# A ring with a copied head, and a maximum that is written back in place

## The chip, the cores and the metric

The kernel runs on one core of one Trainium2 chip. The metric is the device time of one execution in microseconds, lower is better. The core has five engines with a queue each: TensorE for matrix products (PE, with its weight loads shown apart as PEld), VectorE (DVE), ScalarE (ACT), GpSimd (POOL) and SyncE (SP). In this kernel SP does no arithmetic: its queue issues every DMA, one after the other, in the order of the program, and an issue that has to wait holds up all issues behind it.

## The reference

Two branches read the same input `x` (2048 tokens, 512 features, 32-bit floats) and a sigmoid gate per token mixes them.

```python
# attention branch, H = 32 heads of 16, window W = 256
q, k, v = split(x @ wqkv)
scores = q @ k.T * 16 ** -0.5
mask = (i - j >= 0) & (i - j < 256)
o = softmax(where(mask, scores, -1e9)) @ v
a = o @ wo
# gated branch, F = 1376
b = (sigmoid(x @ w_gate) * (x @ w_up)) @ w_down
g = sigmoid((x * gate_w).sum(-1))
out = g * a + (1 - g) * b
```

## The kernel before

**Precision.** Each 32-bit operand is split into a high and a low part, and a product is made of three matrix products, high by high, high by low and low by high. For the projections they are three passes. For the scores they are folded into one pass: the 64 rows of one head in a stack hold 16 rows for each of four terms. Row group 0 of a query block carries minus the row maximum and of a key block the constant one; groups 1 to 3 hold high and low parts of queries and keys (three pairings).

**The ring.** `ring_t` (lines 95 and 96) holds three stacks (`RING = 3`) of 8 blocks of 128 tokens each, 24 blocks. A free index of four says which of queries (0, 1) and keys (2, 3) and which pair of heads; the two heads of a pair lie in rows 0 to 63 and 64 to 127. Stacks are numbered t = 0 to 15. There are eight groups of four heads with 16 blocks each, so a group has two stacks, and stack t lies in third t % 3 of the ring. `stack_build` (line 287) lists 13 DMAs for a stack: one that zeroes the rows of the maximum, and 12 that copy high and low parts from two staging tiles, 32 rows each, first the eight of the high parts and then the four of the low parts.

**Units.** The loop of line 657 runs over units u = 0 to 139. Up to u = 127, unit u is block u % 16 of group u // 16. For each of four heads hh, `s_part` (line 317) multiplies the query block with the key blocks u-2 to u into PSUM, and one DVE instruction adds the mask and takes the maximum per row (line 332); its elementwise result goes to the tile `junk`, which nobody reads, and the maximum to `mx`. The PSUM tile has the tag `s`, of which there are two. `st_part` (line 366) does the same with keys and queries swapped, nine units later (`LAG`), with the maximum in row group 0, and ACT takes the exponential. `pv_burst` makes the product with `v` every four units. Between the heads, `run_slots` puts in the matrix products of the gated branch and of later projections (lines 563 to 576), so that PE has something to do at every point. All engines but POOL run in the order of the program text.

**The cut.** Because the ring has 24 blocks, a run of three blocks can cross its end. `pieces` (line 306) cuts it there, and `s_part` and `st_part` then make two matmuls with the same weights. That is the case at u = 24 and 25, 72 and 73, 120 and 121 for the scores, and nine units after the two blocks before each of these crossings for the transposed ones (block 22 comes up in `st_part` at u = 31, block 23 at u = 32).

**The order of the DMAs.** At u = 10 and then at every u with u % 8 == 1 from 17 on, the variable `sdma` is set to the list of stack u // 8 + 1 (line 673). In each unit the program emits, in this order: the reload of `v` or of projection weights, the load of maxima (`max_load`, where u % 4 == 1), the stores that the unit before left in `later`, then up to three (`SD = 3`) DMAs of `sdma` (lines 674 to 682), and then the heads. In units with u % 4 == 0 the four stores of the maxima (`max_store`, line 717) come after the third head; they wait for a transpose on DVE, and the `max_load` of the next unit waits for these stores to land, since it reads them back from memory.

**After the attention.** The softmax sums are stored, read back into the tile `sm` (line 623, two buffers), inverted on DVE and stored again as `rec_scratch`, once per quarter of the tokens. The loads of the quarters are emitted at u = 127, 131, 135 and 139. The last loads of the sums, of the gate row (line 745) and of the hidden blocks (`h_load`, line 600) stand in one row on the SP queue, and the final stage, lines 788 to 830, begins with the hidden blocks.

Of the kernel before, what the change touches and what calls it, by code (L numbers as in the profile page):

```python
# [7 lines left out]
F32 = mybir.dt.float32  # L8
F32R = mybir.dt.float32r
# [5 lines left out]
P = 128  # L15
# [25 lines left out]
NEG = -1.0e30  # L41

RING = 3
CH2 = 2 * CH
LAG = 9
PVLAG = LAG + 2
SD = 3
QB = 32
# [10 lines left out]
def gated_mix_kernel(  # L59
# [11 lines left out]
    nc = tc.nc  # L71
    ctx.enter_context(tc.manual_schedule(engines={E.PE, E.Activation, E.SP, E.DVE}))

    mm = nc.tensor.matmul
# [15 lines left out]
    max_d = nc.dram_tensor("max_scratch", (NG * NC, HG, 2, 4, P), F32, kind="Internal").ap()  # L90
    fill_d = nc.dram_tensor("fill_scratch", (2, CH2), F32, kind="Internal").ap()

    cpool = ctx.enter_context(tc.tile_pool(name="cpool", bufs=1))
    ps = ctx.enter_context(tc.tile_pool(name="ps", bufs=1, space=PSUM))
    ring_t = cpool.tile([P, 4, RING * CH2], F32R, name="ring")
    ring = [ring_t[:, :, r * CH2:(r + 1) * CH2] for r in range(RING)]
    gsum = cpool.tile([P, NB], F32, name="gsum")
    gs = cpool.tile([P, NB], F32, name="gs")
# [3 lines left out]
    def ring_f(f):  # L102
        t = ring[(NP - 3 + f // 4) % RING]
        return t[:, f % 4, 0:D], t[:, f % 4, D:]
# [24 lines left out]
    with ExitStack() as actx:  # L129
        apool = actx.enter_context(tc.tile_pool(name="apool", bufs=1))  # L130
        xh = apool.tile([P, ND, T], F32R, name="xh")
        xl = apool.tile([P, ND, T], F32R, name="xl")
        w0 = apool.tile([P, 2, CH2], F32R, name="w0")

# [5 lines left out]
        spool = actx.enter_context(tc.tile_pool(name="spool", bufs=2))  # L140
# [35 lines left out]
        def fill_rows(r, which, v):  # L176
            dst = ring[r].bitcast(F32).rearrange("(a r) j f -> r a j f", r=32)[0, :, 2 * which:2 * which + 2]
            return dst, fill_d[v:v + 1].partition_broadcast(8).rearrange("(a j) o f -> a j (o f)", j=2)

        warm = cpool.tile([P, CH2], F32R, tag="hb", name="warm", bufs=4)  # L180
        nc.vector.memset(warm[:, 0:2 * P].bitcast(F32), 0.0)
# [19 lines left out]
        mask = apool.tile([P, 3 * P], F32, name="mask")  # L201
# [8 lines left out]
        )  # L210
        fr = cpool.tile([P, CH2], F32, tag="hb", name="fr", bufs=4)
        nc.gpsimd.memset(fr[0:33], 0.0)
        nc.gpsimd.memset(fr[32:33], 1.0)
        nc.sync.dma_start(fill_d, fr.rearrange("(a r) f -> r a f", r=32)[0, 0:2])
        for r in range(RING):
            nc.gpsimd.memset(ring[r].bitcast(F32), 0.0)
            nc.sync.dma_start(*fill_rows(r, 1, 1))

        def fill_v(b0, b1):
            nc.gpsimd.memset(Vh[:, b0:b1, :, DH:VW], 1.0)  # L220

        fill_v(0, NB // 2)

        vp = {}
# [62 lines left out]
        def stack_build(t):  # L287
            sh, sl = (v.bitcast(F32) for v in stg.pop(t))
            rt = ring[t % RING].bitcast(F32)
            st = rt.rearrange("(a r) j f -> r a j f", r=4)  # L290
            dmas = [fill_rows(t % RING, 0, 0)]
            for low in range(2):
                for j in range(4):
                    for r in range(3):
                        if low == (r == (1 if j < 2 else 2)):
                            dmas.append((st[r + 1, :, j], (sl if low else sh)[32 * j:32 * j + 32]))
            return dmas

        def run_dmas(dmas):
# [2 lines left out]

        def pos(g, b):
            return (g * NB + b) % (8 * RING)

        def pieces(g, b0, b1):
            cut = b0 + 8 * RING - pos(g, b0)
            return [(b0, b1)] if cut >= b1 else [(b0, cut), (cut, b1)]

        def blk(g, b, hh, which, n=1):  # L310
            base = 64 * (hh % 2)
            o = pos(g, b) * P
            return ring_t[base:base + 64, which * 2 + hh // 2, o:o + n * P]
# [3 lines left out]
        def s_part(u, hh):  # L317
            g, i = divmod(u, NB)
            s = g * NC + i // 4
            if i % 4 == 0 and hh == 0:  # L320
                mxs[s] = spool.tile([P, HG, 4], F32, tag="mx", name=f"mx{s}")
            k0 = max(0, i - 2)
            pt = ps.tile([P, 3 * P], F32, tag="s", name=f"s{u}_{hh}", bufs=2)
            lhsT = blk(g, i, hh, 0)
            for k, e in pieces(g, k0, i + 1):
                mm(  # L326
                    pt[:, (k - k0) * P:(e - k0) * P], lhsT, blk(g, k, hh, 1, e - k),
                    start=k == k0, stop=e == i + 1, skip_group_check=True,
                )
            n = (i + 1 - k0) * P  # L330
            junk = spool.tile([P, 3 * P], F32, tag="junk", name=f"junk{u}_{hh}", bufs=2)
            nc.vector.tensor_tensor_reduce(  # L332
                junk[:, 0:n], pt[:, 0:n], mask[:, 3 * P - n:], scale=1.0, scalar=NEG,
                op0=ALU.add, op1=ALU.max, accum_out=mxs[s][:, hh, i % 4:i % 4 + 1],
            )

# [20 lines left out]
        def max_load(s):  # L357
            st = ring[s // 2 % RING].bitcast(F32).rearrange("(a r) j f -> r a j f", r=QB)
            o = s % 2 * CH
            nc.sync.dma_start(  # L360
                st[0, :, 0:2, o:o + CH], max_d[s].rearrange("(p s) l b t -> (s l) p (b t)", p=2),
            )

        pts = {}

        def st_part(u, hh):
            g, j = divmod(u, NB)
            if u not in pts:
                o = PSLOT[u] * PW
                pts[u] = region[:, o:o + PW].rearrange("p (h q) -> p h q", h=HG)  # L370
            tag, bufs = ("s", 2) if u + LAG >= NU else ("st", 3)
            pt = ps.tile([P, 3 * P], F32, tag=tag, name=f"st{u}_{hh}", bufs=bufs)
            lhsT = blk(g, j, hh, 1)
            last = min(NB, j + 3)
            for q, e in pieces(g, j, last):
                mm(  # L376
                    pt[:, (q - j) * P:(e - j) * P], lhsT, blk(g, q, hh, 0, e - q),
                    start=q == j, stop=e == last, skip_group_check=True,
                )
            n = (last - j) * P  # L380
            nc.scalar.activation(pts[u][:, hh, 0:n], pt[:, 0:n], AF.Exp, scale=SCALE)  # L381

        def mask_p(u):
# [87 lines left out]
        proj(0)  # L471
        proj(1)
        run_dmas(stack_build(0))
        split_x(2)
        split_wqk(1, raw_q)
        v_block(4)
        split_x(3)
        fill_v(NB // 2, NB)
        v_block(5)
        proj(2)  # L480
        v_block(6)
        proj(3)
        run_dmas(stack_build(1))
        v_block(7)
        v_block(8)
# [132 lines left out]
        sm = {}  # L618

        def flat(v, c):  # L620
            return v[c].rearrange("h (q t) -> (h q) t", t=P)

        def sums_load(c):
            sm[c] = cpool.tile([P, P], F32, tag="sm", name=f"sm{c}", bufs=2)
            nc.sync.dma_start(sm[c], flat(sum_d, c))

        def sums_invert(c):
# [23 lines left out]
        while w < NU:  # L651
            n = BURST if w + 8 < NU else 2
# [4 lines left out]
        for u in range(N):  # L657
# [15 lines left out]
            if (u % 8 == 1 and u > 16 or u == LAG + 1) and u // 8 + 1 < NP:  # L673
                sdma = stack_build(u // 8 + 1)
            if u % 16 == 8 and u // 16 + 2 < NG:
                raw_q = load_wqk(u // 16 + 2)
            if u % 4 == 1 and 1 < u <= NU + 1:
                max_load(u // 4 - 1)
# [17 lines left out]
            for hh in range(HG):  # L696
                if hh == 0 and u % 2 == 0:
                    if u in bursts:
                        pv_burst(*bursts[u])
                if hh == 0:  # L700
                    head = min(2, bursts.get(u, (0, 0))[1] // 2)
                    run_slots(head)
                if u < NU:
                    s_part(u, hh)
                if 0 <= u - LAG < NU:
                    st_part(u - LAG, hh ^ 1 if u < NU else hh)
                if u < LAG:
                    flush(behind)
                    run_slots(GAP)
                    flush(acts)  # L710
                    flush(behind)
                else:
                    if behind:
                        behind.pop(0)()
                    if acts:
                        acts.pop(0)()
                if hh == 2 and u % 4 == 0 and 0 < u <= NU:
                    max_store(u // 4 - 1)
                if u >= LAG:
                    run_slots((GAP if u >= NU else GAPS[u % 4][hh] if u > LAG + 2 else GAP * (u % 2 == 0 or hh < HG - 1)) - (hh < head))  # L720
# [10 lines left out]
            if SUMS <= u and (u - SUMS) % 4 == 0:  # L731
                sums_load((u - SUMS) // 4)
# [55 lines left out]
        for n, (c, f) in enumerate(steps):  # L788
# [31 lines left out]
            for t in range(4):  # L820
                b = 4 * c + t
# [61 lines left out]
```

## Time and profile before

| | |
|---|---|
| time, median of 3 runs | 728.19 us (727.78 to 728.48) |
| time of the profiled execution | 728.12 us |
| its span, first to last instruction | 726.4 us |
| PE busy | 720.6 us, 99% |
| PEld busy | 594.1 us, 82% |
| DVE busy | 461.2 us, 63% |
| ACT busy | 438.0 us, 60% |
| POOL busy | 166.9 us, 23% |
| mean granted TensorE clock | 0.999 |
| DMA packets | 88,656 on SP's queue, 111.39 MB |

The span leaves out 1.7 us of the profiled execution's own time, before the first and after the last instruction. PE runs two matmuls at once, each on half of the rows, and their records overlap, so the busy time says that there is nearly always a matmul under way and not that each one runs as fast as it can. How long a piece of work takes on PE is therefore read from the distance between starts.

### The profile page before, as it was taken

The numbers are of one execution on the slowest core, as the hardware profiler recorded it, in microseconds if no ns is written. First come the engines' busy times: TensorE is split into PE (matmuls) and PEld (weight loads), VectorE is DVE, ScalarE is ACT, GpSimd is POOL, SyncE is SP. The second block draws the span as 40 slices with busy tenths as digits, with TensorE's granted clock in tenths as the row PEclk, the third lists the DMA queues.
The fourth block names the chain that finished last, engine by engine and source line by source line (L and its number), as shares of the span: only waits on it lengthen the run. The fifth ranks groups of instructions, "written<-read, shape, count | busy, mean of one in ns | idle before, by whom it ended". The sixth has DMA issues, their size and how long they took to land.

```text
span 726.4 us, 20432 instructions
## 1 busy us (share of the span) xinstructions
PE 720.6 (99%) x7775; PEld 594.1 (82%) x7775; DVE 461.2 (63%) x1426; ACT 438.0 (60%) x899; POOL 166.9 (23%) x256
## 2 busy tenths in 40 slices
PE   9999999999999999999999999999999999999997
PEld 7888788888888878878888788888886788888886
DVE  4447867757776676766776677666415868557471
ACT  6412876667677677667667677666767545435241
POOL 7000433332233233232323323323330000000000
PEclk9999999999999999999999999999999999999999
DMA  9382564445455355345545435644464959366441
GB/s 319 97 267 85 144 167 136 137 133 139 125 151 136 109 148 156 120 122 154 137 129 135 134 100 151 187 134 151 151 187 144 272 188 276 126 227 190 150 138 58
DMA packets 88753, 112.68 MB, mean 155 GB/s; under 512 B 36050, under 2 KB 45778, under 8 KB 88656
## 3 DMA queue, kind: packets, MB, share of 16 engines
q1 hardware_dynamic: 88656, 111.39, 52.2%
q8 instruction: 61, 1.00, 0.6%
q14 instruction: 36, 0.29, 0.1%
HBM read 49.72 MB, written 36.45 MB: 119 GB/s over the span
## 4 chain that ended last, share of the span: by engine, by line
PE 96%; DMA 1%; DVE 1%; SPq 0%; issue 0%; ACT 0%; DVEq 0%; ACTq 0%
PE gu L259 38%; PE pj L259 10%; PE pvs L430 8%; PE st L376 6%; PE s L326 6%; PE pd L83 5%; PE pd L81 5%; PE pd L82 5%; PE vps L241 3%; PE pa L81 2%; PE pa L83 2%; PE pa L82 2%; PE pvst L430 2%; PE vps L82 1%; PE vps L83 1%; PE vps L81 1%
## 5 line engine op out<-in xcount | busy, mean ns | idle before, releaser
L332 DVE CUSTOM_DVE_ANT_0 junk<-s,mask 128x384 f32<-128x384 f32 (+2 forms) x512 | 267.5, 530 | 148.3 <-PE st L376 91.6
L259 PE MATMUL gu<-xh,w 64*128 64x512 f32 (+2 forms) x1392 | 357.7, 395 | 0.0
L381 ACT ACTIVATE region<-st 128x384 f32<-128x384 f32 (+2 forms) x512 | 242.4, 476 | 92.1 <-PE st L376 42.1
L259 PE MATMUL gu<-xl,w 64*128 64x512 f32 (+2 forms) x696 | 247.1, 393 | 0.0
L259 PEld LDWEIGHTS gu<-xh,w 64*128 64x128 f32 (+2 forms) x1392 | 203.1, 183 | 22.4 <-issue 6.9
L386 POOL TENSOR_SCALAR_AFFINE_SELECT region<-region 128x512 f32<-128x512 f32 x128 | 85.5, 668 | 369.9 <-ACT region L381 283.9
L376 PE MATMUL st<-ring 64*128 64x384 f32 (+2 forms) x536 | 167.6, 320 | 0.0
L326 PE MATMUL s<-ring 64*128 64x384 f32 (+2 forms) x536 | 167.1, 321 | 0.5 <-DVE mx L332 0.5
L259 PEld LDWEIGHTS gu<-xl,w 64*128 64x128 f32 (+2 forms) x696 | 123.2, 183 | 6.3 <-issue 0.6
L326 PEld LDWEIGHTS s<-ring 64*128 64x128 f32 x536 | 98.4, 184 | 22.0 <-DVE mx L332 12.8
L376 PEld LDWEIGHTS st<-ring 64*128 64x128 f32 x536 | 98.3, 184 | 7.1 <-ACT region L381 0.2
L259 PE MATMUL pj<-xl,wqh 64*128 64x512 f32 (+1 forms) x240 | 95.2, 402 | 0.0
L259 PE MATMUL pj<-xh,wqh 64*128 64x512 f32 (+1 forms) x240 | 93.3, 394 | 0.0
L259 PE MATMUL pj<-xh,wql 64*128 64x512 f32 (+1 forms) x240 | 75.0, 392 | 0.0
L430 PE MATMUL pvs<-region,vg 64*32 64x320 f32 (+4 forms) x1440 | 73.4, 345 | 0.0
L391 POOL TENSOR_SCALAR_AFFINE_SELECT region<-region 128x512 f32<-128x512 f32 x112 | 71.9, 642 | 0.0
L430 PE MATMUL pvst<-region,vg 64*32 64x320 f32 (+4 forms) x1440 | 71.7, 340 | 0.0
L83 PE MATMUL pd<-ring,hb 128*128 128x512 f32 (+1 forms) x176 | 69.1, 392 | 0.3 <-DVE hb L78 0.3
L81 PE MATMUL pd<-ring,hb 128*128 128x512 f32 (+1 forms) x176 | 69.3, 394 | 0.0
L82 PE MATMUL pd<-ring,hb 128*128 128x512 f32 (+1 forms) x176 | 68.5, 389 | 0.0
L430 PEld LDWEIGHTS pvs<-region,vg 64*32 64x32 f32 x1440 | 45.1, 106 | 26.4 <-issue 4.0
L77 ACT CAST hb<-region 128x512 fp32r<-128x512 f32 (+1 forms) x37 | 23.0, 621 | 50.0 <-DVE region L616 41.3
(83 smaller groups left out, 1031.3 us busy)
## 6 DMA issues: line engine op xcount, KB each, us to landing
gu_scratch<-sp SPq DMA_DIRECT2D x80, 256.0 KB
region<-gu_scratch SPq DMA_DIRECT2D x68, 256.0 KB
ring<-sh SPq DMA_DIRECT2D x128, 128.0 KB
ring<-sl SPq DMA_DIRECT2D x64, 128.0 KB
guraw<-in_wgu_dram SPq DMA_DIRECT2D x20, 256.0 KB
v_scratch<-region SPq DMA_DIRECT2D x16, 272.0 KB
vg<-v_scratch SPq DMA_DIRECT2D x8, 544.0 KB
region<-in_xT_dram SPq DMA_DIRECT2D x16, 256.0 KB
```

The costliest lines, as they stand in the source:

```text
L77: nc.scalar.copy(hi, src)
L81: mm(ps, lh, rh, start=first, stop=False)
L82: mm(ps, lh, rl, start=False, stop=False)
L83: mm(ps, ll, rh, start=False, stop=last)
L259: mm(pt[0:fw], (wl if w == 2 else wh)[r, d], (xl if w == 1 else xh)[r, d, c * CH:(c + 1) * CH], start=k == 0 and half != 1, stop=k == 3 * ...
L326: mm(pt[:, (k - k0) * P:(e - k0) * P], lhsT, blk(g, k, hh, 1, e - k), start=k == k0, stop=e == i + 1, skip_group_check=True,)
L332: nc.vector.tensor_tensor_reduce(junk[:, 0:n], pt[:, 0:n], mask[:, 3 * P - n:], scale=1.0, scalar=NEG, op0=ALU.add, op1=ALU.max, accum_out ...
L376: mm(pt[:, (q - j) * P:(e - j) * P], lhsT, blk(g, q, hh, 0, e - q), start=q == j, stop=e == last, skip_group_check=True,)
L381: nc.scalar.activation(pts[u][:, hh, 0:n], pt[:, 0:n], AF.Exp, scale=SCALE)
L386: nc.gpsimd.affine_select(p[:, :, 0:P], p[:, :, 0:P], pattern=[[0, HG], [1, P]], compare_op=ALU.is_ge, fill=0.0, base=0, channel_multiplie ...
L391: nc.gpsimd.affine_select(p[:, :, 2 * P:], p[:, :, 2 * P:], pattern=[[0, HG], [-1, P]], compare_op=ALU.is_gt, fill=0.0, base=0, channel_mu ...
L430: mm(acc[half][32 * hh:32 * hh + 32, q0:q1], vg[g % 2][r, c:c + 32], pts[g * NB + j][r, hh, q0 + o:q1 + o], start=m == 0, stop=m == len(or ...
```

## The change

The ring gets 256 more columns behind its end (`EXT`), which hold a second copy of its first two blocks. `pieces` goes away: a run of three blocks is always one matmul, and where it crosses the end it reads on into the copy. The copy is filled whenever a stack that begins the ring anew in the middle of a group is built (t = 3, 9 and 15): 12 more DMAs of 32 rows by 256 columns, behind the 13 of that stack in the same list. The maxima of the two blocks get one more load each time (`max_load` at u = 29, 77 and 125). POOL clears the copy once at the start.

To make room, `junk` goes: the DVE instruction of line 332 writes its elementwise result over the PSUM tile that it reads. And the tile `sm` has one buffer in place of two.

```diff
+EXT = 2 * P
...
-    ring_t = cpool.tile([P, 4, RING * CH2], F32R, name="ring")
+    ring_t = cpool.tile([P, 4, RING * CH2 + EXT], F32R, name="ring")
...
+        ext = ring_t[:, :, RING * CH2:].bitcast(F32)
+        nc.gpsimd.memset(ext, 0.0)
...
                     for r in range(3):
                         if low == (r == (1 if j < 2 else 2)):
                             dmas.append((st[r + 1, :, j], (sl if low else sh)[32 * j:32 * j + 32]))
+            if t % RING == 0 and t % 2:
+                se = ext.rearrange("(a r) j f -> r a j f", r=4)
+                for low in range(2):
+                    for j in range(4):
+                        for r in range(3):
+                            if low == (r == (1 if j < 2 else 2)):
+                                dmas.append((se[r + 1, :, j], (sl if low else sh)[32 * j:32 * j + 32, 0:EXT]))
             return dmas
...
-        def pieces(g, b0, b1):
-            cut = b0 + 8 * RING - pos(g, b0)
-            return [(b0, b1)] if cut >= b1 else [(b0, cut), (cut, b1)]
...
-            for k, e in pieces(g, k0, i + 1):
-                mm(
-                    pt[:, (k - k0) * P:(e - k0) * P], lhsT, blk(g, k, hh, 1, e - k),
-                    start=k == k0, stop=e == i + 1, skip_group_check=True,
-                )
             n = (i + 1 - k0) * P
-            junk = spool.tile([P, 3 * P], F32, tag="junk", name=f"junk{u}_{hh}", bufs=2)
+            mm(pt[:, 0:n], lhsT, blk(g, k0, hh, 1, i + 1 - k0), start=True, stop=True)
             nc.vector.tensor_tensor_reduce(
-                junk[:, 0:n], pt[:, 0:n], mask[:, 3 * P - n:], scale=1.0, scalar=NEG,
+                pt[:, 0:n], pt[:, 0:n], mask[:, 3 * P - n:], scale=1.0, scalar=NEG,
                 op0=ALU.add, op1=ALU.max, accum_out=mxs[s][:, hh, i % 4:i % 4 + 1],
             )
...
+            if s % (4 * RING) == 2 * RING:
+                se = ext.rearrange("(a r) j f -> r a j f", r=QB)
+                nc.sync.dma_start(
+                    se[0, :, 0:2], max_d[s, :, :, 0:2].rearrange("(p s) l b t -> (s l) p (b t)", p=2),
+                )
...
-            for q, e in pieces(g, j, last):
-                mm(
-                    pt[:, (q - j) * P:(e - j) * P], lhsT, blk(g, q, hh, 0, e - q),
-                    start=q == j, stop=e == last, skip_group_check=True,
-                )
             n = (last - j) * P
+            mm(pt[:, 0:n], lhsT, blk(g, j, hh, 0, last - j), start=True, stop=True)
...
-            sm[c] = cpool.tile([P, P], F32, tag="sm", name=f"sm{c}", bufs=2)
+            sm[c] = cpool.tile([P, P], F32, tag="sm", name=f"sm{c}", bufs=1)
```

## The prediction

> **What bounds the kernel now.** I read the page first (span, busy times, the chain that ended last), then PE's waits, then the timelines of PE and SP around the three crossings of the ring's end.
>
> ```profile
> span 726.4 us, 20432 instructions
> ...
> PE 96%; DMA 1%; DVE 1%; SPq 0%; issue 0%; ACT 0%; DVEq 0%; ACTq 0%
> ```
> ```profile
> PEld s L326 <- DVE mx L332: 12.8, 54, 0.9
> ```
>
> PE carries 96% of the chain. Any time in which PE stands still is added to the end, and only what shortens PE's own row of work can be won. The third line, of the list of waits, is the largest wait on PE's side: 54 weight loads of a score matmul wait for the DVE maximum to free a PSUM tile, 12.8 us in all, mostly under matmuls already running.
>
> **What the undivided matmuls save.** Units with the same u % 16 have the same work, so a unit with a cut can be set against one without. PE starts of the first score matmul of units 24 and 26, 40 and 42, 31 and 33, 47 and 49:
>
> ```profile
> 124.10 0.27 PE L326 MATMUL s<-ring 64*128 64x256 f32 x1
> 133.20 0.33 PE L326 MATMUL s<-ring 64*128 64x384 f32 x1
> 184.11 0.33 PE L326 MATMUL s<-ring 64*128 64x384 f32 x1
> 193.00 0.33 PE L326 MATMUL s<-ring 64*128 64x384 f32 x1
> 150.96 0.44 PE L326 MATMUL s<-ring 64*128 64x384 f32 x1
> 157.64 0.28 PE L326 MATMUL s<-ring 64*128 64x256 f32 x1
> 210.73 0.44 PE L326 MATMUL s<-ring 64*128 64x384 f32 x1
> 217.25 0.27 PE L326 MATMUL s<-ring 64*128 64x256 f32 x1
> ```
>
> Units 24 and 25 hold eight cut scores and take 9.10 us; 40 and 41 hold none and take 8.89: 0.21 us. Units 31 and 32 hold eight cut transposed scores and take 6.68 us; 47 and 48 take 6.52: 0.16 us. That is 0.37 us for a crossing and **1.1 us** for three. It is all that the removal of 48 matmuls and 48 weight loads is worth, 0.02 us each, since the columns streamed stay the same.
>
> **What the copy's DMAs cost.** A list of 25 DMAs issued three to a unit no longer ends where 13 did. For t = 3 it starts at u = 17: numbers 0 to 12 (the old ones) are issued by u = 21, where 13 and 14 follow, 15 to 17 at u = 22, 18 to 20 at u = 23, 21 to 23 at u = 24. Number 23 is the low part of the keys of heads 0 and 1 (j = 2, r = 2). The first score matmul of u = 24 reads keys 22 to 24, and key block 24 is now read from the copy. So **it has to wait for a DMA that is emitted just before it**, while block 24 in the ring itself was complete with number 12. (At u = 25 and 73 `sdma` is set anew, so number 24 is never issued for t = 3 and 9; one low part of the copy stays zero there, in scores that only choose a maximum. For t = 15 it goes out at u = 121.)
>
> When does it land? The SP queue at units 21 to 25:
>
> ```profile
> 118.20 0.49 SPq L301 DMA_DIRECT2D ring<-sl  x1
> 118.79 0.54 SPq L301 DMA_DIRECT2D gu_scratch<-sp  x1
> 119.73 1.72 SPq L301 DMA_DIRECT2D oT_scratch<-ob  x4
> 121.49 0.56 SPq L301 DMA_DIRECT2D sum_scratch<-ob  x1
> 122.10 0.43 SPq L146 DMA_DIRECT2D wqraw<-in_wqk_dram  x1
> 123.48 0.34 SPq L301 DMA_DIRECT2D gu_scratch<-sp  x1
> 126.91 1.92 SPq L355 DMA_DIRECT2D max_scratch<-nt  x4
> 130.37 0.59 SPq L360 DMA_DIRECT2D ring<-max_scratch  x1
> ```
>
> The first row is number 12, and SP is already late there, since PE began unit 24 at 124.10, only 5.9 us later. The issue price of a ring DMA, from six in a row:
>
> ```profile
> 109.05 1.77 SPq L301 DMA_DIRECT2D ring<-sh  x3
> 110.86 1.88 SPq L301 DMA_DIRECT2D ring<-sl  x3
> 112.79 0.59 SPq L499 DMA_DIRECT2D guraw<-in_wgu_dram  x1
> ```
>
> (112.79 - 109.05) / 6 = 0.62 us each; the new ones have the same 32 strided rows and a quarter of the bytes, and I take the same (a bound below is 0.5, the 0.49 of number 12 alone). Landing: the store of the maxima ends its issue at 126.91 + 1.92 = 128.83, and the load that waits for it starts at 130.37, so 1.5 us. Number 23 is in place at 118.20 + 0.5 (number 12) + 11 x 0.62 = 6.8 (numbers 13 to 23) + 3.8 (the five groups between, with gaps of 0.05) + 1.5 = 130.8. PE stands from 124.10 to 130.8: **6.7 us**. Nothing else can run on PE, because its queue is in order. The other two crossings, number 12 and the first cut score:
>
> ```profile
> 296.80 0.49 SPq L301 DMA_DIRECT2D ring<-sl  x1
> 303.63 0.27 PE L326 MATMUL s<-ring 64*128 64x256 f32 x1
> 476.26 1.09 SPq L301 DMA_DIRECT2D ring<-sl  x1
> 483.15 0.27 PE L326 MATMUL s<-ring 64*128 64x256 f32 x1
> ```
>
> Both have a weight load of the gated branch more between, 0.5 us: 0.5 + 6.8 + 4.3 + 1.5 - 6.83 = **6.3 us**, and 1.1 + 6.8 + 4.3 + 1.5 - 6.89 = **6.8 us**.
>
> The third crossing waits again. Number 24 (keys of heads 2 and 3) is emitted at u = 121, behind the load of the maxima, and the third head of that unit needs it:
>
> ```profile
> 488.17 0.22 PE L326 MATMUL s<-ring 64*128 64x128 f32 x1
> 490.28 0.86 SPq L301 DMA_DIRECT2D gu_scratch<-sp  x2
> ```
>
> SP gets there 491.14 - 483.15 = 8.0 us after the start of unit 120, since the store of the maxima in between waits for PE and DVE; with 0.6 to issue and 1.5 to land that is 10.1 us, and PE wants it after 488.17 - 483.15 = 5.0: **5.1 us**. The four waits are 6.7 + 6.3 + 6.8 + 5.1 = 24.9 us. What stands behind PE (DVE maxima, ACT exponentials, stores) only moves along.
>
> **The clock after a wait.** A PE that has stood still comes back slower. The warm-up matmuls at the start, a run of twice as wide matmuls at full speed, and the clock at the end:
>
> ```profile
> 1.25 4.09 PE L184 MATMUL warm_ps<-warm 128*128 128x256 f32 x19 [1.25 <-DVE warm L181]
> ```
> ```profile
> 16.42 5.44 PE pj L259 x24
> ```
> ```profile
> 722.00:723.00 1.00, 0.67 (x3) 0.21 (x2) 0.22 (x1) 0.00 (x0) 0.00 (x0) 1.00 0.37 141
> 725.00:726.00 1.00, 0.00 (x0) 0.00 (x0) 0.00 (x0) 0.00 (x0) 0.00 (x0) 0.50 0.07 27
> ```
>
> 256 columns took 4.09 / 19 = 0.215 us at first and 512 columns take 5.44 / 24 = 0.227 later: half speed for about 4.1 us of work. And between 2.3 and 3.3 us after the last matmul (it ends at 722.67) the granted clock is 0.50. All four waits are longer than that, so each costs another 4.1 / 2 = 2.0 us: **8.0 us**, between none and twice as much. [...]
>
> **The rest.** The write to PSUM: no DVE instruction of this trace writes there, so the nearest rows are one with its source in SBUF and in PSUM, below the row of the maximum itself:
>
> ```profile
> L332 DVE CUSTOM_DVE_ANT_0 junk<-s,mask 128x384 f32<-128x384 f32 x448 | 244.8, 555 | 125.0 <-PE st L376 85.1 <-PE s L326 32.2 <-PE vps L241 0.8
> L285 DVE TENSOR_TENSOR sl<-pr,sh 128x512 fp32r<-128x512 f32 x28 | 19.3, 689 | 1.0 <-ACT sh L281 0.9
> L285 DVE TENSOR_TENSOR sl<-pj,sh 128x512 fp32r<-128x512 f32 x4 | 2.8, 693 | 14.4 <-ACT sh L281 12.2 <-issue 2.2
> ```
>
> The place makes 4 ns there. At 4 ns on the 54 releases that PE waits for, 0.2 us; I take **0**. Faster, it can win at most the part of those waits that is not hidden, which I bound at 1 us; if each operation took a tenth of its 555 ns longer (some 50 ns), 54 x 0.05 = 2.7 us, up to 7 with the backlog. [...]
>
> One buffer for `sm`: the load of the last quarter now waits until the stored reciprocals of the one before have been read out.
>
> ```profile
> 561.17 0.39 SPq L301 DMA_DIRECT2D rec_scratch<-sm  x1
> 562.28 0.32 SPq L625 DMA_DIRECT2D sm<-sum_scratch  x1
> 574.68 0.50 PE L83 MATMUL pd<-ring,hb 128*128 128x512 f32 x1 [0.34 <-DVE hb L78]
> ```
>
> 561.17 + 0.39 + 1.5 = 563.1, so the load and the hidden-block loads behind it go out 0.8 us later, and PE already waits for a hidden block at 574.68. Between 0 (the DMA engines are busy there) and 0.8; I take **0.6**. POOL's memset of the copy lies before a wait of POOL that the list puts at 11 us:
>
> ```profile
> 25.67 0.58 POOL L220 MEMSET region<- 128x256 f32 x1 [10.98 <-DVE xl L78]
> ```
>
> A quarter of a ring third's memset is about 1 us, hidden there; without that cover it would be 1 us of POOL, not of PE. The extra loads of maxima (0.6 us of SP at u = 29, 77, 125) are needed two units later, 6 us or more, and cost nothing.
>
> **Sum:** 24.9 + 8.0 - 1.1 + 0.6 + 0 = +32.4 us on the profiled execution's own 728.1 us (span 726.4 and 1.7 around it; the median is 728.19, the same): **760.5 us**, 4.4% slower.
>
> **Rivals.** (1) *The copies are in place in time.* Then only the cut matmuls and `sm` count: 728.1 - 1.1 + 0.6 = 727.6, no difference. It needs number 23 landed by 124.10; against it, number 12 itself was only issued at 118.20, and eleven issues do not fit into 5.9 us with the stores between. It decides for this rival if SP were 6.7 us ahead of where the rows show it. 6%. (2) *DVE frees PSUM sooner* because the write no longer goes through SBUF, and the copies are in time: 728.1 - 1.1 - 1 + 0.6 = 726.6. For it speak the 54 waits, against it the 4 ns. Faster by just 0.2%: 4%. (3) *The write to PSUM is the whole story*, copies in time: 727.6 + 2.7 to 7, about 732. 4%. [...] 20%. The forecast as summed has 66%.
>
> **How the numbers follow.** 66% + 20% wait for the copy, and both are slower; so is (3): slower 90%, within 0.2% (about what this kernel's runs can tell) 6%, faster 4%. For the range, the waits with 0.5 us per issue are 3 x 11 x 0.12 = 4 us shorter and with (4) give 748; shorter landings and a free DMA queue could take another 1.5 us from each wait, 742. Above, twice the clock loss gives 768. Range 742 to 769.
>
> **What would show it.** Score and transposed matmuls fall from 536 to 512 each; issues `ring<-sh` rise from 128 to 152 and `ring<-sl` from 64 to 74. PE's waits have a new row, the score matmul behind DMA `ring<-sl`, three times 6 to 7 us and once 5, at about 124, 312 and 500 us of the span; behind each, the granted clock is 0.5 for some 4 us. Units 31 and 32 take 6.52 us. [...] A mean of the DVE group of line 332 away from 555 ns for 384 columns would show (2) or (3), and a larger wait of PE near the hidden blocks the term of `sm`.

## The result

The changed kernel takes **765.3 us** (median of 6 runs, 763.17 to 768.95) where the kernel before takes 728.62 in the same call (727.78 to 730.08): a ratio of 1.0503, 95% interval 1.0482 to 1.0523, **36.7 us slower**. The prediction was 760.5 us, in a range of 742 to 769. The profiled execution of the changed kernel took 763.17 us with a span of 761.5, 35.1 more than the span before.

From the page of the changed kernel: its span, the clock in 40 slices, and the group of the score matmuls (busy time, mean ns of one, idle time before them and what ended most of it).

```profile
span 761.5 us, 20335 instructions
...
PEclk9999998999999999899999999989999999999999
...
L333 PE MATMUL s<-ring 64*128 64x384 f32 (+2 forms) x512 | 170.8, 336 | 25.1 <-DMA ring<-sl 24.5
```

The score matmuls are 512 in place of 536, as the change says, and they have a wait that did not exist before: 24.5 us behind a DMA from the staging tile of the low parts into the ring. The clock dips in three slices, at about 125, 315 and 510 us. The list of PE's waits says how often, and the timelines of PE and SP say where:

```profile
PE s L333 <- DMA ring<-sl: 24.5, 4, 7.6
```

```profile
132.10 0.65 PE L333 MATMUL s<-ring 64*128 64x384 f32 x1 [6.93 <-DMA ring<-sl]
142.57 0.33 PE L333 MATMUL s<-ring 64*128 64x384 f32 x1
321.36 0.66 PE L333 MATMUL s<-ring 64*128 64x384 f32 x1 [7.04 <-DMA ring<-sl]
332.58 0.33 PE L333 MATMUL s<-ring 64*128 64x384 f32 x1
512.12 0.66 PE L333 MATMUL s<-ring 64*128 64x384 f32 x1 [7.64 <-DMA ring<-sl]
522.54 0.41 PE L333 MATMUL s<-ring 64*128 64x384 f32 x1 [2.89 <-DMA ring<-sl]
526.69 0.33 PE L333 MATMUL s<-ring 64*128 64x384 f32 x1
```

```profile
118.91 0.49 SPq L312 DMA_DIRECT2D ring<-sl  x1
119.45 1.23 SPq L312 DMA_DIRECT2D ring<-sh  x2
120.73 0.58 SPq L312 DMA_DIRECT2D gu_scratch<-sp  x1
121.36 1.75 SPq L312 DMA_DIRECT2D ring<-sh  x3
123.21 1.92 SPq L312 DMA_DIRECT2D oT_scratch<-ob  x4
125.16 0.56 SPq L312 DMA_DIRECT2D sum_scratch<-ob  x1
125.77 1.99 SPq L312 DMA_DIRECT2D ring<-sh  x3
127.81 0.57 SPq L147 DMA_DIRECT2D wqraw<-in_wqk_dram  x1
128.49 0.37 SPq L312 DMA_DIRECT2D gu_scratch<-sp  x1
128.90 1.77 SPq L312 DMA_DIRECT2D ring<-sl  x3
```

The first row of SP is number 12 of the list, and below it stand the eleven new issues in groups of two, three, three and three. The last ends at 130.67, and PE starts 1.43 us later, at 132.10, after 6.93 us in which it did nothing. The first score matmul after the wait takes 0.65 us where one of its shape takes 0.33 at unit 26 (the second row). The clock, in windows that split the first crossing (busy times of PE, PEld, DVE, ACT and POOL, granted clock, DMA share, GB/s):

```profile
128.00:132.00 4.00, 0.00 (x0) 0.00 (x0) 0.00 (x0) 0.00 (x0) 0.00 (x0) 0.54 0.51 164
132.00:135.00 3.00, 2.90 (x16) 2.72 (x18) 1.31 (x6) 0.56 (x2) 0.00 (x0) 0.50 0.02 5
135.00:138.00 3.00, 3.00 (x32) 2.73 (x30) 2.02 (x8) 2.08 (x5) 0.64 (x1) 0.98 0.02 3
```

For the first 3 us after the wait PE ran 16 matmuls, and 32 in the next 3. The second cost is on DVE:

```profile
L334 DVE CUSTOM_DVE_ANT_0 s<-s,mask 128x384 f32<-128x384 f32 x448 | 250.2, 568 | 143.6 <-PE st L383 80.9 <-PE s L333 59.1
L334 DVE DVE_READ_ACCUMULATOR2_ANT mx<- 128x1 f32 x512 | 72.6, 142 | 0.0
```

The second of these rows in the kernel before:

```profile
L332 DVE DVE_READ_ACCUMULATOR2_ANT mx<- 128x1 f32 x512 | 42.3, 83 | 0.0
```

The instruction that writes in place takes 568 ns where it took 555, and the read of its accumulator that follows, 142 where it took 83 in the kernel before. Together that is 72 ns per tile and 512 x 72 = 36.9 us of DVE.

That number is a trap: 36.9 is almost exactly the 36.7 us by which the kernel got slower. So there were two theories: one that explained most of the difference from the waits and the clock, and one that seemed to explain all of it from DVE alone.

### The profile page after: what moved, and what is told of

Its sections match the earlier page's. It is cut to its first block, busy times and chain, and to the rows that moved or that the text cites. A ratio compares the mean times of both kernels' runs of the same rounds, so it can differ in the third digit from the quotient of the medians.

```text
span 761.5 us, 20335 instructions
## 1 busy us (share of the span) xinstructions
PE 730.4 (96%) x7727; PEld 603.6 (79%) x7727; DVE 479.3 (63%) x1426; ACT 437.9 (58%) x899; POOL 168.3 (22%) x257
## 4 chain that ended last, share of the span: by engine, by line
PE 93%; SPq 3%; DMA 2%; DVE 1%; issue 1%; ACT 0%; DVEq 0%
PE gu L263 35%; PE pj L263 10%; PE pvs L433 8%; PE s L333 6%; PE st L383 5%; PE pd L84 5%; PE pd L82 5%; PE pd L83 5%; PE vps L245 3%; SPq L312 2%; PE pa L82 2%; PE pa L84 2%; PE pa L83 2%; PE pvst L433 2%; PE vps L83 1%; PE vps L82 1%
## 5 line engine op out<-in xcount | busy, mean ns | idle before, releaser
L334 DVE CUSTOM_DVE_ANT_0 s<-s,mask 128x384 f32<-128x384 f32 (+2 forms) x512 | 273.4, 543 | 164.6 <-PE st L383 84.0
L263 PE MATMUL gu<-xh,w 64*128 64x512 f32 (+2 forms) x1392 | 361.4, 398 | 0.0
L263 PEld LDWEIGHTS gu<-xh,w 64*128 64x128 f32 (+2 forms) x1392 | 208.1, 185 | 21.8 <-issue 6.9
L333 PE MATMUL s<-ring 64*128 64x384 f32 (+2 forms) x512 | 170.8, 336 | 25.1 <-DMA ring<-sl 24.5
L383 PE MATMUL st<-ring 64*128 64x384 f32 (+2 forms) x512 | 170.5, 333 | 0.0
L333 PEld LDWEIGHTS s<-ring 64*128 64x128 f32 x512 | 95.4, 187 | 50.9 <-issue 26.5
L383 PEld LDWEIGHTS st<-ring 64*128 64x128 f32 x512 | 95.6, 187 | 6.1 <-ACT region L384 0.2
L334 DVE DVE_READ_ACCUMULATOR2_ANT mx<- 128x1 f32 x512 | 72.6, 142 | 0.0
L433 PEld LDWEIGHTS pvs<-region,vg 64*32 64x32 f32 x1440 | 48.2, 106 | 24.6 <-DVE mx L334 5.5
```

The source lines that it names most:

```text
L263: mm(pt[0:fw], (wl if w == 2 else wh)[r, d], (xl if w == 1 else xh)[r, d, c * CH:(c + 1) * CH], start=k == 0 and half != 1, stop=k == 3 * ...
L333: mm(pt[:, 0:n], lhsT, blk(g, k0, hh, 1, i + 1 - k0), start=True, stop=True)
L334: nc.vector.tensor_tensor_reduce(pt[:, 0:n], pt[:, 0:n], mask[:, 3 * P - n:], scale=1.0, scalar=NEG, op0=ALU.add, op1=ALU.max, accum_out=m ...
L383: mm(pt[:, 0:n], lhsT, blk(g, j, hh, 0, last - j), start=True, stop=True)
L433: mm(acc[half][32 * hh:32 * hh + 32, q0:q1], vg[g % 2][r, c:c + 32], pts[g * NB + j][r, hh, q0 + o:q1 + o], start=m == 0, stop=m == len(or ...
```

## The experiments

**Theory A** was the prediction's: PE waits for the copy and comes back at half speed. **Theory B**: DVE's 36.9 us. Three of the first four runs tell them apart.

### Only the in-place write

```diff
# the kernel before
-            junk = spool.tile([P, 3 * P], F32, tag="junk", name=f"junk{u}_{hh}", bufs=2)
...
-                junk[:, 0:n], pt[:, 0:n], mask[:, 3 * P - n:], scale=1.0, scalar=NEG,
+                pt[:, 0:n], pt[:, 0:n], mask[:, 3 * P - n:], scale=1.0, scalar=NEG,
```

> The kernel before, with only the in-place write: the DVE instruction of line 332 writes its elementwise result over its PSUM tile. Theory A: the DVE pair becomes 72 ns longer as in the changed kernel, but DVE is not the bound, and only the releases for which PE already waits move: 728.6 + 2 to 3 us = about 731 us. Theory B: near 765 us.

Measured 732.12 us against 728.53, ratio 1.0057 (1.0040 to 1.0074): 3.6 us by the medians, between 2.9 and 5.4 by the interval. DVE's durations are those of the changed kernel (569 and 142 ns), so the full 36.9 us of DVE are there, and some nine tenths of them cost nothing. Theory B falls. What they do cost shows where PE's weight loads wait for the maximum:

```profile
PEld s L326 <- DVE mx L331: 16.6, 62, 1.0
```

62 waits and 16.6 us, where the kernel before had 54 and 12.8.

### Matmuls in the waits

```diff
# the kernel after
             n = (i + 1 - k0) * P
+            for _ in range({(24, 0): 40, (72, 0): 40, (120, 0): 44, (121, 2): 17}.get((u, hh), 0)):
+                mm(pt, xh[:, 0, 0:P], xh[:, 1, 0:3 * P], start=True, stop=True)
             mm(pt[:, 0:n], lhsT, blk(g, k0, hh, 1, i + 1 - k0), start=True, stop=True)
```

> The kernel after, with matmuls that nobody reads in front of the four score matmuls that wait for the copy: 40, 40 and 44 at units 24, 72 and 120 (about 0.16 us each, so some 6.5 to 7 us) and 17 in front of the third head of unit 121, into the PSUM tile that the score matmul then overwrites. The waits stay filled with work, so the copy lands as late as before. Theory A: the granted clock stays at 1.00; the records of the changed kernel show half speed from 128.3 to 135.1, 319.4 to 326.3 and 507.2 to 517.4 us, of which PE worked some 3, 5 and 5 us, so 6.6 us come back: 765.3 - 6.6 = about 759 us. If the clock costs nothing beside the wait: 765 us. Theory B: 765 us or more.

Measured 762.52 us, ratio 1.0463 (1.0446 to 1.0481); the mean granted clock was 0.999 where the changed kernel has 0.983.

```profile
125.63 7.22 PE L334 MATMUL s<-xh 128*128 128x384 f32 x40
133.09 0.41 PE L335 MATMUL s<-ring 64*128 64x384 f32 x1 [0.24 <-DMA ring<-sl]
```
```profile
PE s L335 <- DMA ring<-sl: 2.8, 4, 1.7
```

141 matmuls more, and the kernel is not slower but by its ratio some 0.4% faster, 2.9 us, since PE did not lose its clock. That is less than the 6.6 us expected. The added matmuls (141, together 25.6 us) and the wait that is left (2.8) make 28.4 us where the wait alone was 24.5. Half of these 3.9 us lie at the third crossing. The first row is the last issue of the copy for unit 120 in the changed kernel, the other two are the same issue and the score matmul behind it in this run:

```profile
508.80 1.76 SPq L312 DMA_DIRECT2D ring<-sl  x3
```
```profile
509.03 1.76 SPq L312 DMA_DIRECT2D ring<-sl  x3
512.11 0.44 PE L335 MATMUL s<-ring 64*128 64x384 f32 x1 [1.74 <-DMA ring<-sl]
```

PE reached the last score of unit 119 at 501.72 here and at 503.66 in the changed kernel, 1.9 us earlier. The copy was issued no earlier, and unit 120 began at 512.11 against 512.12. So SP set the time of this crossing, and PE waited away what it had won at the first two. This run confirms the sign and that the dip follows from PE's idleness.

What the clock costs where it drops is read better from the changed kernel's own rows. From the first score of unit 24 (72, 120) to that of unit 26 (74, 122) it takes 142.57 - 132.10 = 10.47, 11.22 and 14.57 - 2.89 = 11.68 us, where the kernel before took 9.10 at the first crossing (its rows stand in the prediction) with the cut matmuls, which made 0.21 of it. Over 3 x 8.89 us that is **6.7 us**. Against the same units of the run with two DMAs and the in-place write below (8.99, 8.91 and 8.99 us) it is 6.5; the 0.2 between them is the in-place write's.

### The copy in time

```diff
# the kernel after
-                for low in range(2):
-                    for j in range(4):
+                for j in (2, 3, 0, 1):
+                    for low in range(2):
...
-            run_dmas(sdma[:SD])
-            del sdma[:SD]
+            sd = 5 if u % 24 >= 17 else SD
+            run_dmas(sdma[:sd])
+            del sdma[:sd]
```

> The kernel after, with the copies of the keys listed before those of the queries and five DMAs of a list issued per unit in the eight units in which a list has a copy in it, so that the key copies are issued by unit 20, 68 and 116. Theory A (PE waits for the copy, and the clock drops behind the waits): the four waits of 24.5 us and the clock's loss go, and what stays is the slower DVE write (units longer by some 0.06 us, about 2 us), 0.6 us of the single sums buffer and 1.1 us won: 728.6 + 2 + 0.6 - 1.1 = about 730 us. Theory B (the write to PSUM is the cause: the DVE pair of line 332 takes 568 + 142 ns in place of 555 + 83, and 512 x 72 ns = 36.9 us, which is the whole difference): the time stays near 765 us.

Measured **748.24 us**, ratio 1.0267 (1.0239 to 1.0296): neither 730 nor 765. The wait for the copy is gone from the list of PE's waits, and another has come:

```profile
PE st L383 <- DMA ring<-max_scratch: 10.9, 4, 5.4
```
```profile
139.49 0.41 PE L383 MATMUL st<-ring 64*128 64x384 f32 x1 [1.44 <-DMA ring<-max_scratch]
```
```profile
132.30 1.81 SPq L357 DMA_DIRECT2D max_scratch<-nt  x4
137.24 0.57 SPq L362 DMA_DIRECT2D ring<-max_scratch  x1
```

At unit 27 the transposed scores need the maxima that `max_load` fetches at unit 25. SP stores them at 132.30 and issues the load at 137.24, where the kernel before did so at 126.91 and 130.37; PE began unit 24 at 125.62 here and at 124.10 there, so only 1.5 us of the delay are PE's own. Twelve issues of 0.62 us are 7.4 us of SP's time. The kernel before had less than that to spare: ahead of this store SP waited 3.0 us for DVE. In this order the maxima are late in place of the copy. Not all of it is issuing: from the end of the store to the load it takes 3.1 us here and 1.5 in the kernel before, and why is not shown.

The waits make 10.9 of the 18.9 us between the spans (745.3 and 726.4) and the in-place write 3.6; behind one of the waits the granted clock was 0.55 for 3 us, so a part of the rest is the clock. Theory A was right on the place of the loss and wrong on its remedy. **Theory C**: the copy costs the time of its issues on SP's queue, and which wait this becomes depends on the order.

### The copy made, but not read

```diff
# the kernel after
         def blk(g, b, hh, which, n=1):
             base = 64 * (hh % 2)
-            o = pos(g, b) * P
+            o = min(pos(g, b), 8 * RING - n) * P
```

> The kernel after, but the two matmuls read their three blocks from the last three of the ring where they would cross its end, so that nobody reads the copy (the scores of these units are of other blocks than the reference's). All DMAs of the copy are issued at the same places as before. Theory A as first put (the cost is the wait for the copy): no wait is left, 728.5 - 1.1 + 0.6 + 3.5 (the write to PSUM, from the run with that alone) = about 731.5 us. Theory C, from the run with the keys first (the copy was in time there and PE waited for maxima instead): SP's queue has no room for 12 issues of 0.62 us, 7.4 us, and the maxima that are read back come late; PE then waits for them for some 2 to 6 us at each crossing, about 740 to 748 us.

Measured 737.09 us against 729.64, ratio 1.0107 (1.0092 to 1.0122). It lies between the two: 7.5 us, of which the in-place write makes 3.6 and the missing cuts give back 1.1, so some 5 us are due to DMAs whose data nobody reads. PE waits only at the third crossing, and again for the maxima:

```profile
502.01 0.41 PE L383 MATMUL st<-ring 64*128 64x384 f32 x1 [2.36 <-DMA ring<-max_scratch]
```

Theory C holds in kind, but the first two crossings absorbed the issues here, so its number (740 to 748) was too high. With the issues spread over four units as in the changed kernel, SP nearly catches up; with five to a unit from unit 17 on, as in the run before, it does not. At the first crossing the load of the maxima goes out at 133.22 here, 1.2 us after the end of their store, and at 137.24 there, 3.1 us after it, with PE 1.0 us later. What makes the landing so different was not tested.

### The copy by two DMAs

If the number of issues is the cost, the copy can be made from the ring itself, once the stack is complete.

```diff
# the kernel after, without the twelve DMAs in stack_build
+            if u % 48 in (22, 23):
+                js = slice(2, 4) if u % 48 == 22 else slice(0, 2)
+                nc.sync.dma_start(ext[:, js], ring_t[:, js, 0:EXT].bitcast(F32))
             run_dmas(sdma[:SD])
```

It was run with the in-place write and with an 8-bit result in SBUF (one buffer).

> The kernel after with only the copy made otherwise: two DMAs from the ring itself at units 22 and 23, 70 and 71, 118 and 119 in place of twelve from the staging tiles. The in-place write and the one buffer for the sums stay. Theory C (the twelve issues and the wait behind them are the loss): of the changed kernel's 36.7 us only the in-place write's 3.5 us stay, less 1.1 for the cuts, 728.6 + 2.4 = about 731 us, a ratio of 1.003. If the read from the copy itself cost anything, more.

Measured 732.35 us against 729.21, ratio 1.0035 (1.0022 to 1.0048): 3.1 us, of the 36.7. No wait for `ring` is left on PE. This is the changed kernel with another way to fill the copy and nothing else, so **the way it is filled makes over 30 of the 36.7 us**, and reading from the copy adds nothing that can be told from the 1.003 expected without it. Bytes are not the cause: the two DMAs move 512 KB at a crossing, the twelve 384. The number of issues, their place in the queue and their source changed together; that the number decides is argued from the run with the copy in time, where another order of the twelve only moved the wait.

> The ring with its copy, but the copy made by two DMAs in place of twelve: after the stack is complete, the two blocks of keys are copied from the ring itself (one DMA at units 22, 70 and 118), those of the queries one unit later; the maxima as in the kernel after. The elementwise result of line 332 goes to 8-bit integers in SBUF as in the run before. SP gets 3 issues more at each crossing, 1.8 us, in place of 13. Theory C: neither PE nor the maxima wait, 728.5 - 1.1 + 0.6 = about 728 us, up to 730 if the 8-bit result holds PE up a little. Theory A as first put says the same. If a copy of 256 KB lands later than the score matmul of unit 24 wants it (2 us from the issue are there), PE waits up to 1 us there.

Measured 733.59 us against 729.64, ratio 1.0065 (1.0049 to 1.0081). The waits are gone and it is still 4 us or so too slow. DVE's single instruction is back at 556 ns and the accumulator's read at 83, but the group's busy time is not:

```profile
L328 DVE CUSTOM_DVE_ANT_0 junk<-s,mask 128x384 uint8<-128x384 f32 x448 | 249.0, 556 | 124.2 <-PE st L377 72.7 <-PE s L326 19.1
```

249.0 us, all of 448 x 0.556 = 249.1, where the same 448 instructions at 555 ns filled 244.8 of 248.6 in the kernel before: the records no longer overlap. With one buffer each instruction starts only after the one before has ended: of two in a row the second starts 0.71 us behind the first (201.06 and 201.77), where with the two buffers of the run further below it can start after 0.48 (210.76 and 211.24; in the kernel before, 211.67 and 212.15), while the first still runs. The same with 8 bits and one buffer, but with the twelve DMAs, keys first and five to a unit:

> The kernel with both costs removed: the ring with its copy, keys first and five DMAs per unit, and the elementwise result of line 332 back in SBUF, as 8-bit integers in one buffer (nobody reads it; the three kilobytes that a 32-bit tile took are not there beside the copy). Theory A: 728.6 - 1.1 + 0.6 = about 728.1 us, the DVE instruction at 555 ns. Theory B: the same, about 728 us. If the conversion to 8 bits makes the DVE instruction longer, the time lies nearer to 730 us.

Measured 752.13 us, ratio 1.0315 (1.0283 to 1.0346). Both theories said 728: it has the late maxima of the run with the copy in time (a wait of 12.0 us in all for them), and this single buffer on top. So the run could not have told A and B apart; it shows the single buffer once more (249.0 us).

### Two buffers

```diff
# the run before last (two copies, 8 bits)
-            junk = spool.tile([P, 3 * P], mybir.dt.uint8, tag="junk", name=f"junk{u}_{hh}", bufs=1)
+            junk = spool.tile([P, 3 * P], mybir.dt.uint8, tag="junk", name=f"junk{u}_{hh}", bufs=2)
...
-            sm[c] = cpool.tile([P, P], F32, tag="sm", name=f"sm{c}", bufs=1)
+            sm[c] = mask[:, c % 3 * P:c % 3 * P + P]
```

> The run with the two copies, with two buffers for the 8-bit result in place of one; the room comes from the sums, which are inverted in the mask's memory (nobody reads the mask after unit 127). Theory D (the 4 us that the run with the two copies was still longer come from its single buffer for the result, which makes each DVE maximum wait for the end of the one before): the units are as long as in the kernel before but for the crossings, and the time is that of the run without cuts, 1.1 us under the kernel before, a ratio of 0.9985. Theory E (8 bits or the copies themselves cost it): about 1.006, as with one buffer.

Measured 728.70 us against 729.21, ratio 0.9994 (0.9982 to 1.0006).

```profile
L328 DVE CUSTOM_DVE_ANT_0 junk<-s,mask 128x384 uint8<-128x384 f32 x448 | 244.9, 556 | 124.6 <-PE st L377 85.1 <-PE s L326 32.2 <-PE vps L245 0.7
```

244.9 us again: theory D holds, it was the single buffer and not the 8 bits. (The sums in the mask's memory are the other edit; one buffer for them cost nothing that can be measured, as the last run below shows.) This is the ring with its copy at no cost, and it is **not to be told from the kernel before**; the interval holds the expected 0.9985 and holds 1.

### What the cuts and the sums buffer are worth

```diff
# the kernel before, two runs
         def pieces(g, b0, b1):
-            cut = b0 + 8 * RING - pos(g, b0)
-            return [(b0, b1)] if cut >= b1 else [(b0, cut), (cut, b1)]
+            return [(b0, b1)]
...
-            o = pos(g, b) * P
+            o = min(pos(g, b), 8 * RING - n) * P

-            sm[c] = cpool.tile([P, P], F32, tag="sm", name=f"sm{c}", bufs=2)
+            sm[c] = cpool.tile([P, P], F32, tag="sm", name=f"sm{c}", bufs=1)
```

> The kernel before with undivided matmuls and no copy: where three blocks cross the ring's end, the last three blocks of the ring are read instead (the scores of these units are of other blocks than the reference's). 48 matmuls and 48 weight loads fewer, nothing else changed. By the unit times of the kernel before, 0.37 us for a crossing: 728.5 - 1.1 = 727.4 us. If the removed matmuls had cost their full duration (48 x 0.22 us), 718 us.

Measured a ratio of 0.9985 (0.9974 to 0.9996) over 11 runs: 1.1 us, between 0.3 and 1.9, on 729.64.

> The kernel before with only the one buffer for the sums. The load of the last quarter waits for the reciprocals of the one before to be stored, 0.8 us, and PE's wait for a hidden block in the last stage grows from 0.3 to at most 1.1 us: 728.5 + 0.6 = 729.1 us, between 728.5 and 729.3.

Measured a ratio of 0.9999 (0.9990 to 1.0008): nothing that can be measured, at most 0.7 us won and 0.6 lost.

## Why the prediction was right

**The waits for the copy.** Predicted 6.7, 6.3, 6.8 and 5.1 us; measured 6.93, 7.04, 7.64 and 2.89, together 24.5 against 24.9. Three hold to within 0.9 us, each a little longer. At the first crossing it took 11.76 us from the start of number 12 to the end of number 23 where 11.1 was worked out, and the landing 1.43 where 1.5 was taken. The fourth is 2.2 us too long in the prediction. Its place of SP was measured from the start of unit 120 at full speed, but unit 120 ran at half speed, so PE came later to the third head of unit 121 and had less to wait. The prediction had the clock's loss as a term of its own and did not carry it into the wait behind it.

**The clock.** Predicted 8.0 us, 2.0 for each of four waits; measured 6.7 by the rows of units 24 to 26 and their like, and not in four parts: 1.6, 2.3 and 2.8 us behind the first three waits, and nothing behind the fourth, where the granted clock stays at 1.00:

```profile
519.00:522.50 3.50, 0.65 (x8) 0.22 (x4) 0.62 (x2) 0.49 (x1) 0.00 (x0) 1.00 0.25 89
524.00:527.00 3.00, 3.00 (x104) 2.14 (x86) 0.52 (x2) 1.09 (x3) 1.22 (x2) 1.00 0.59 177
```

That the sum came near is luck in part: the prediction charged one dip too many, and the later dips were longer than it allowed. Half speed ended at 135.1, 326.3 and 517.4, so PE worked at it for 3.0, 4.9 and 5.3 us, where 4.1 was taken from the durations of the warm-up matmuls. (The granted clock of that stretch, the first 4 us of the kernel before, reads 1.00, so the view of the clock does not confirm the 4.1.)

The chance of 20% that the waits come but the clock stays up did not come true: the granted clock is 0.50 when PE resumes from the first three waits. The (4) of the prediction's range is this case, 760.5 - 8.0 = 752.5 us; no run shows the clock staying up behind a wait as long as these three. A shorter wait was enough to lose it: in the run whose copy nobody reads, one of 2.36 us, ended at 502.01.

```profile
502.00:503.00 1.00, 0.99 (x10) 1.00 (x12) 0.00 (x0) 0.48 (x2) 0.00 (x0) 1.00 0.66 223
503.00:506.00 3.00, 3.00 (x19) 3.00 (x18) 1.71 (x5) 1.40 (x4) 0.00 (x0) 0.52 0.84 259
```

The clock drops a microsecond after PE has resumed, from 1.00 to 0.52. The changed kernel's fourth wait, 2.89 us, cost nothing (1.00), and in the profiled execution of the run with keys first and 8 bits, waits of up to 2.7 us passed with a granted clock of 1.00 throughout (its three other executions had 0.991 to 0.993). So of waits between 2.3 and 2.9 us one cost the clock and others did not; what decides it was not shown.

**The cuts.** Predicted 1.1 us for 48 matmuls, 0.02 us each, by units with and without; the run without them measured 1.1. Setting a unit against its like in another group, which does the same work, gave this; the run's interval, 0.3 to 1.9 us, cannot confirm it to a tenth.

**The write to PSUM** is the term that was mis-sized: taken as 0, it measured 3.6 us (in the bounds of -1 to 7). The step that failed is "the nearest rows are one with its source in SBUF and in PSUM". A source in PSUM cost 4 ns (693 against 689); a destination there costs 13 ns on the instruction and 59 on the accumulator's read behind it, which no row of the trace before could tell, and the read was left out of the term altogether.

**The sums buffer** was taken as 0.6 us and is not to be told from 0 on its own.

The terms as measured, 24.5 + 6.7 + 3.6 - 1.1 = 33.7 us, leave 1.4 of the 35.1 us between the two spans. 0.5 of it is a longer wait for a hidden block in the last stage (0.80 us against 0.34); the rest is not assigned. In the prediction's sum the errors partly cancel: 2.2 us too much for the fourth wait and 1.3 for the clock stand against 3.6 too little for the write to PSUM and 1.8 for the first three waits.

**The rivals.** That the copies are in place in time fell with the first timeline; what decided it was named rightly, that SP is late before the new issues begin. The rival's price of 727.6 us holds only for a copy that needs few issues: with two DMAs, and the result of the maximum in SBUF, it was 728.70. With the twelve issued in time it was 748, of which the in-place write makes 3.6. The time of twelve issues on a queue that runs late has to come from somewhere, and the prediction priced them only up to the DMA that PE waits for, while the stores and loads of the maxima behind them were among what "only moves along". In the changed kernel they did: at the first crossing PE stood still for 6.93 us, and behind it SP waited 5.6 us for DVE ahead of the next store of the maxima, so it had caught up. In the run whose copy nobody reads they did so at two crossings of three without PE standing still.

## What to carry to other kernels

When DMAs are added to a queue that issues everything, first look how far that queue is behind the engine it feeds at that point, and price each issue, not its bytes: here 0.6 us each, 12 of them, on a queue that had some 3 us to spare at the next store. Then follow every deadline behind the new issues, not just their own: here a wait taken away by another order came back at the next deadline, and went when twelve issues became two. And when a cost summed over an engine that is not the bound happens to equal the whole loss, that engine's change alone is the run to make first.

## What the runs showed that was not expected

A DVE maximum with an accumulator is slower with its elementwise result in PSUM: 568 in place of 555 ns for 384 columns, and its accumulator's read 142 in place of 83 ns, and so in the runs with only the in-place write, with the matmuls in the waits and with the copy in time (568 to 569 and 142 ns). An 8-bit result in SBUF costs nothing (556 and 83 ns), but one buffer in place of two for a result that nobody reads costs about 5 us over 512 instructions (1.0065 against 0.9994). And a copy of 256 columns of 1 KB rows by 32 strided partitions takes SP as long to issue as one of 4 KB rows, 0.59 us, while one DMA of all 128 partitions and two kilobytes a partition takes 0.65 to 0.69 us and replaces six. A PE that waited for 2.4 us was granted 0.52 of its clock for 3 us, beginning a microsecond after it had resumed; one that waited for 2.9 us kept 1.00.
